# Short matrix products placed between long ones in a gated attention and MLP kernel

## The chip, the cores and the metric

The kernel runs on one core of one Trainium2 chip. The metric is the device time of one execution in microseconds (us). Before the change it is 208.64 us, the median of 3 runs (208.62 to 208.71). The profile shows one execution, which took 208.87 us; the span in its records, from first to last instruction, is 207.1 us.

## What is computed

Two branches over the same 2048 rows of 512 values are mixed by a gate per row. Branch A is linear attention with 32 heads of 16, whose features are softmaxes; branch B is a gated MLP whose second half is mixed over the rows.

```python
# A: B, S, D, H = 1, 2048, 512, 32; Dh = 16
q, k, v = split(x @ wqkv)                       # each (heads, 2048, 16)
pq, pk  = q @ w_phi, k @ w_phi                  # per head, 16 x 16
phi_q = concat([softmax(pq), softmax(-pq)])     # (heads, 2048, 32)
phi_k = concat([softmax(pk), softmax(-pk)])
kv  = einsum('bhsf,bhsd->bhfd', phi_k, v)       # the key sums
z   = einsum('bhsf->bhf', phi_k)
num = einsum('bhqf,bhfd->bhqd', phi_q, kv)      # the query sums
den = einsum('bhqf,bhf->bhq', phi_q, z)[..., None] + 1e-06
a   = (num / den) @ wo
# B: F = 1376, Fh = 688
zB = gelu(x @ w_in)
g  = w_sp @ layernorm(zB[..., Fh:]) + b_sp      # w_sp is 2048 x 2048
b  = (zB[..., :Fh] * g) @ w_out
gate = sigmoid((x * gate_w).sum(-1))
out  = gate * a + (1 - gate) * b
```

## The kernel before

The rows are cut into 16 tiles of 128. All matrix products accumulate in one PSUM tensor `ps` of 8 banks, each 128 x 512 in FP32. The order of work on every engine is the order in which the program writes it: there is no scheduler, each engine works through its own instructions in order and waits at semaphores where data is needed.

The stages, with their places in the profile:

1. Up to 59 us: x is transposed, branch B's `zz` (gelu) is formed with `z_piece` (line 180), the values `vv` with `v_proj` (line 282), and w_phi is folded into the key and query weights (`fold`, line 305).
2. 59 to 130 us, the key stage. `gg_half(i)` (line 396) makes half of one row tile of w_sp times zz: 16 products with 344 columns, into bank 0 or 1; VectorE then makes `u` from it (line 404), and a transposing DMA on SyncE's queue makes `uT`. `k_proj(t)` is four products of 512 columns (line 327), then two exponentials on ScalarE (line 333). `k_norm` calls `norm`: on VectorE a sum (line 338), a reciprocal (line 340) and a multiplication of one half (line 342), while GpSimd multiplies the other half. `kv_acc(t)` (line 372) is a block of 8 short products of 65 columns, one for each group of 4 heads, added over all tiles into eight slots (`slots`, banks 3 and 4).
3. 130 to 195 us, the query stage: a loop over `j` = 0 to 15. `gg_at` puts one or two `gg_half` ahead of j = 0, 1, 2, 3, 5, 7, 9, 11, 13 and 14. `q_num(j)` (line 420) is a block of 8 short products of 68 columns, written into the same `slots`; VectorE then takes a reciprocal of the denominators (`rd`, line 424) and writes the quotients times the gate (`o`, line 426), both reading all of `slots`; a transposing DMA makes `oT`. `q_proj(j + 4)` is like `k_proj`; `q_norm(j + 3)` is `norm` and a transposing DMA that makes `eT`, the stationary operand of a later `q_num`. From j = 3 on, `out_tile(j - 3)` adds six products with w_out (line 439) and four with wo (line 444), all of 512 columns; ScalarE copies the result to `ob` (line 448), which is then stored.
4. After the loop the last three out tiles. The very last one is made in two parts of 256 columns, in banks 6 and 7, each with its own copy and store.

There is one set of `slots`. So the first product of `q_num(j + 1)` waits until VectorE has finished `o` of j. In the program before, the loop's body is:

```python
gg(gg_at.get(j, 0))
q_num(j)                      # 8 short products, then rd and o on VectorE
if j + 4 < NT: q_proj(j + 4)
if j + 3 < NT: q_norm(j + 3)  # sum, reciprocal, multiplication on VectorE
if j >= LAG: out_tile(j - LAG)
```

Of the kernel before, what the change touches and what calls it, by code (L numbers as in the profile page):

```python
# [14 lines left out]
P = 128  # L15
S = 2048
D = 512
# [5 lines left out]
NT = S // P  # L23
NDT = D // P
# [6 lines left out]
NHG = 8  # L31
HW = 4 * DH
VP = HW + 2
QW = HW + 4
WSLOTS = 8
LAG = 3
# [3 lines left out]
def kernel(  # L40
# [14 lines left out]
    nc = tc.nc  # L55
# [9 lines left out]
    ps = psp.tile([P, 8, CH], FP32, name="ps")  # L65
# [5 lines left out]
    xT = pers.tile([P, NDT, S], BF16, name="xT")  # L71
    w_in = pers.tile([P, NDT, F + 1], BF16, name="w_in")
    wv = pers.tile([P, NDT, D], BF16, name="wv")
    wq = pers.tile([P, NDT, D], BF16, name="wq")
    wk = pers.tile([P, NDT, D], BF16, name="wk")
# [4 lines left out]
    vv = pers.tile([P, NT, NHG, VP], BF16, name="vv")  # L80
    wsp = pers.tile([P, WSLOTS, NT, P], BF16, name="wsp")
    kvx = pers.tile([P, NHG, QW], BF16, name="kvx")
# [59 lines left out]
    def load_wsp(t):  # L142
        nc.sync.dma_start_transpose(
            out=wsp[:, t % WSLOTS, :, :], in_=B_w_sp[t * P:(t + 1) * P, :]
        )
# [166 lines left out]
    KBANK = (2, 6)  # L312
    QBANK = (5, 7)
    ek_t = {}
    eq_t = {}
    w_in_flat = w_in[:].rearrange("p d f -> p (d f)")

    def e_slot(i):
        if i == 5:
            flat = xn[:].rearrange("p t d -> p (t d)")  # L320
        else:
            flat = w_in_flat[:, i * 2 * D:(i + 1) * 2 * D]
        return flat.rearrange("p (g a n) -> p g a n", g=NHG, a=2)

    def feat(t, w, b, e):
        for dt in range(NDT):
            nc.tensor.matmul(  # L327
                ps[:, b, :], lhsT=xT[:, dt, t * P:(t + 1) * P], rhs=w[:, dt, :],
                start=(dt == 0), stop=(dt == NDT - 1),
            )  # L330
        src = ps[:, b, :].rearrange("p (g n) -> p g n", g=NHG)
        for a, sc in enumerate((1.0, -1.0)):
            nc.scalar.activation(out=e[:, :, a, :], in_=src, func=AF.Exp, scale=sc)  # L333
# [12 lines left out]

    def k_proj(t):
        ek_t[t] = e_slot(t % 4)
        feat(t, wk, KBANK[t % 2], ek_t[t])

    def k_norm(t):
        norm(ek_t[t])

    def q_proj(t):
        eq_t[t] = e_slot(4 + t % 2 if t < 4 else (t - 4) % 6)
        feat(t, wq, QBANK[t % 2], eq_t[t])

    eT_t = {}

    def q_norm(t):  # L360
        e = eq_t.pop(t)
        norm(e)
        eT = wqkT[:, 2 * (t % 4):2 * (t % 4) + 2, :].rearrange("p a (b n) -> p (a b) n", n=P)
        nc.sync.dma_start_transpose(out=eT, in_=e.rearrange("p g a n -> p (g a n)"))
        eT_t[t] = eT

    slots = ps[:, 3:5, :].rearrange("p b (c w) -> p (b c) w", w=P)

    def kv_acc(t):
        ek = ek_t.pop(t)  # L370
        for g in range(NHG):
            nc.tensor.matmul(  # L372
                slots[:, g, 0:HW + 1], lhsT=ek[:, g, :, :].rearrange("p a n -> p (a n)"),
                rhs=vv[:, t, g, 0:HW + 1],
                start=(t == 0 and g % 4 == 0), stop=(t == NT - 1), skip_group_check=True,
            )

    def kv_extract():
        nc.vector.tensor_tensor(
# [9 lines left out]

    uT_t = {}  # L390

    def gg_half(i, s0=0, s1=NT):
        tt, h = divmod(i, 2)
        b = i % 2
        for s in range(s0, s1):
            nc.tensor.matmul(  # L396
                ps[:, b, 0:HF], lhsT=wsp[:, tt % WSLOTS, s, :],
                rhs=zz[:, s, FH + h * HF:FH + (h + 1) * HF],
                start=(s == 0), stop=(s == NT - 1),
            )  # L400
        if s1 < NT:
            return
        u = upad[tt % 3]
        nc.vector.scalar_tensor_tensor(  # L404
            out=u[:, h * HF:(h + 1) * HF], in0=ps[:, b, 0:HF], scalar=bcol[:, tt:tt + 1],
            in1=zz[:, tt, h * HF:(h + 1) * HF], op0=ALU.add, op1=ALU.mult,
        )
        if h == 1:
            uT = uTpool.tile([P, NFT, P], BF16, name="uT")
            nc.sync.dma_start_transpose(out=uT[:, :, :], in_=u[:, :])  # L410
            uT_t[tt] = uT
            if tt + WSLOTS < NT:
                load_wsp(tt + WSLOTS)

    oT_t = {}

    def q_num(t):
        eT = eT_t.pop(t)
        for g in range(NHG):
            nc.tensor.matmul(  # L420
                slots[:, g, 0:QW], lhsT=eT[:, g, :], rhs=kvx[:, g, :], start=True, stop=True
            )
        rd = ring2.tile([P, NHG, 4], FP32, name="rd")
        nc.vector.reciprocal(out=rd[:], in_=slots[:, :, HW:QW])
        o = ring2.tile([P, D], BF16, name="o")
        nc.vector.scalar_tensor_tensor(  # L426
            out=o[:].rearrange("p (g h d) -> p g h d", g=NHG, h=4),
            in0=slots[:, :, 0:HW].rearrange("p g (h d) -> p g h d", h=4),
            scalar=gate[:, t:t + 1],
            in1=rd[:, :, :, None].to_broadcast([P, NHG, 4, DH]), op0=ALU.mult, op1=ALU.mult,  # L430
        )
        oT = oTpool.tile([P, NDT, P], BF16, name="oT")
        nc.sync.dma_start_transpose(out=oT[:, :, :], in_=o[:, :])
        oT_t[t] = oT

    def out_part(t, b, n0, n1, ob, dma):
        uT, oT = uT_t[t], oT_t[t]
        for ft in range(NFT):
            nc.tensor.matmul(  # L439
                ps[:, b, n0:n1], lhsT=uT[:, ft, :], rhs=w_out[:, ft, n0:n1],  # L440
                start=(ft == 0), stop=False,
            )
        for g in range(NDT):
            nc.tensor.matmul(  # L444
                ps[:, b, n0:n1], lhsT=oT[:, g, :], rhs=wo[:, g, n0:n1],
                start=False, stop=(g == NDT - 1),
            )
        nc.scalar.activation(out=ob[:, n0:n1], in_=ps[:, b, n0:n1], func=AF.Copy)  # L448
        dma.dma_start(out=out2[t * P:(t + 1) * P, n0:n1], in_=ob[:, n0:n1])

    def out_tile(t):
        ob = ring3.tile([P, D], BF16, name="ob")
        if t < NT - 1:
            out_part(t, (2, 6)[t % 2], 0, D, ob, nc.scalar)
        else:
            out_part(t, 6, 0, D // 2, ob, nc.sync)
            out_part(t, 7, D // 2, D, ob, nc.scalar)

    uTpool = ctx.enter_context(tc.tile_pool(name="uTp", bufs=NT))
    oTpool = ctx.enter_context(tc.tile_pool(name="oTp", bufs=LAG + 2))  # L460
# [39 lines left out]
    for t in range(NT - VLAG, NT):  # L500
        v_proj(t)
    k_proj(0)
    k_proj(1)
    for t in range(NT - 5, NT):
        z1_gate(t)

    gg_next = 0

    def gg(n):
        nonlocal gg_next  # L510
        for _ in range(n):
            gg_half(gg_next)
            gg_next += 1

    Q_AT = {7: 0, 9: 1, 11: 2}
    for i in range(NT):
        gg(1)
        k_norm(i)
        if i >= 2:
            kv_acc(i - 2)  # L520
        if i + 2 < NT:
            k_proj(i + 2)
        if i in Q_AT:
            q_proj(Q_AT[i])
        if i - 1 in Q_AT:
            gg(1)
            q_norm(Q_AT[i - 1])

    q_proj(3)
    gg(2)  # L530
    kv_acc(NT - 2)
    kv_acc(NT - 1)
    kv_extract()
    gg_at = {0: 1, 1: 1, 2: 2, 3: 1, 5: 1, 7: 1, 9: 1, 11: 1, 13: 1, 14: 1}
    for j in range(NT):
        gg(gg_at.get(j, 0))
        q_num(j)
        if j + 4 < NT:
            q_proj(j + 4)
        if j + 3 < NT:  # L540
            q_norm(j + 3)
        if j >= LAG:
            out_tile(j - LAG)
    for j in range(NT - LAG, NT):
        out_tile(j)
# [28 lines left out]
```

## Time and profile before

| what | value |
|---|---|
| median time of 3 runs | 208.64 us (208.62 to 208.71) |
| the profiled execution's own time | 208.87 us |
| its span | 207.1 us, 1.8 us less than its own time |
| TensorE (PE) busy | 202.6 us, 98% of the span, 1399 products |
| VectorE (DVE) busy | 148.5 us, 72% |
| ScalarE (ACT) / GpSimd (POOL) busy | 82.1 us, 40% / 49.5 us, 24% |
| granted TensorE clock | 1.000 |
| short products, 65 and 68 columns | 128 and 128 |

The profile gives for each instruction its start and its duration. Products are pipelined: one has a duration from its start to its result of some 0.2 to 0.4 us, and the next begins long before that. What a product costs TensorE is the distance between two starts; the chain of waits shows this, since it lists how far each group moves the end. The chain's times of a product lie a fraction of a microsecond after the starts that the timeline shows. An instruction on VectorE that depends on nothing close before it can begin a little before the last one's end.

### The profile page before, as it was taken

What the parts mean: (1) busy time and instruction counts of PE and PEld (TensorE: products, weight loads), DVE (VectorE), ACT (ScalarE), POOL (GpSimd) and SP (SyncE); (2) the same over time, 40 slices, a digit from 0 to 9 for tenths busy, and PEclk for the clock granted to TensorE, in tenths of its full rate; (3) what the DMA queues carried; (4) which work ended last, traced back from release to release, by engine and by line L of the source; (5) the groups of instructions that cost most, each with busy time, mean ns of one, the idle gap of its engine ahead of it and who ended that gap; (6) DMA issues with size and microseconds to landing.
All of it is one profiled execution on the core that took longest, in us unless ns stands there. A gap on an engine that the chain in (4) does not pass through costs nothing.

```text
span 207.1 us, 3685 instructions
## 1 busy us (share of the span) xinstructions
PE 202.6 (98%) x1399; PEld 118.2 (57%) x1399; DVE 148.5 (72%) x304; ACT 82.1 (40%) x145; POOL 49.5 (24%) x46
## 2 busy tenths in 40 slices
PE   8899999999999999999999999999999999999994
PEld 7454555555455666666666667666455555555543
DVE  1048858376887988878888996698989778795500
ACT  3266757575684424250505102222524243341122
POOL 4000000000002343525352544032522252322000
DMA  6999899997000634472757771137765963567451
GB/s 188 233 188 255 178 178 227 173 188 234 0 3 0 138 69 112 101 127 67 162 118 112 139 170 41 38 90 76 170 140 119 151 162 80 134 135 164 101 104 51
DMA packets 90378, 26.50 MB, mean 128 GB/s; under 512 B 84168, under 2 KB 90360, under 8 KB 90360
## 3 DMA queue, kind: packets, MB, share of 16 engines
q1 hardware_dynamic: 87360, 23.84, 58.9%
q10 hardware_dynamic: 3000, 2.43, 3.9%
q8 instruction: 11, 0.18, 0.4%
q14 instruction: 7, 0.06, 0.1%
HBM read 3.44 MB, written 2.10 MB: 27 GB/s over the span
## 4 chain that ended last, share of the span: by engine, by line
PE 98%; issue 0%; ACT 0%; DVE 0%
PE ps L396 36%; PE ps L180 18%; PE ps L327 13%; PE ps L439 10%; PE ps L444 7%; PE ps L282 7%; PE ps L420 2%; PE ps L372 2%; PE ps L189 1%; PE ps L305 1%; PE ps L195 0%; ACT ob L448 0%; DVE w_in L212 0%; PE ps L209 0%
## 5 line engine op out<-in xcount | busy, mean ns | idle before, releaser
L396 PE MATMUL ps<-zz,wsp 128*128 128x344 bf16 x512 | 79.1, 310 | 0.0
L342 POOL TENSOR_TENSOR w_in<-w_in,rs 128x512 bf16<-128x512 bf16 x28 | 41.3, 1475 | 124.8 <-DVE rs L340 117.3
L396 PEld LDWEIGHTS <-wsp 128*128 128x128 bf16 x512 | 49.9, 98 | 27.9
L333 ACT ACTIVATE w_in<-ps 128x512 bf16<-128x512 f32 x56 | 30.1, 596 | 63.5 <-issue 21.5
L180 PE MATMUL ps<-w_in,xT 128*128 128x512 bf16 (+2 forms) x200 | 39.8, 350 | 0.7 <-DVE w_in L212 0.7
L338 DVE TENSOR_REDUCE zs<-w_in 128x64 f32<-128x1024 bf16 x28 | 33.8, 1209 | 0.0
L404 DVE SCALAR_TENSOR_TENSOR u<-ps,bcol,zz 128x344 bf16<-128x344 f32 x32 | 18.4, 574 | 18.6 <-PE ps L396 18.5
L180 PEld LDWEIGHTS <-xT 128*128 128x128 bf16 x200 | 18.9, 97 | 18.5 <-DMA w_in<-in_B_w_in_dram 1.0
L215 ACT ACTIVATE zz<-ps 128x1376 bf16<-128x1376 f32 (+2 forms) x18 | 21.4, 1190 | 18.9 <-PE ps L180 18.8
L439 PE MATMUL ps<-w_out,uT 128*128 128x512 bf16 (+1 forms) x102 | 23.5, 367 | 0.0
L224 DVE BATCH_NORM_STATS2 stats<-zz 128x6 f32<-128x344 bf16 x32 | 14.8, 505 | 11.2 <-ACT zz L215 11.2
L342 DVE TENSOR_TENSOR w_in<-w_in,rs 128x512 bf16<-128x512 bf16 x28 | 19.4, 692 | 1.0
L340 DVE RECIPROCAL rs<-zs 128x64 f32<-128x64 f32 x32 | 17.7, 552 | 3.2
L448 ACT ACTIVATE ob<-ps 128x512 bf16<-128x512 f32 (+1 forms) x17 | 9.7, 572 | 25.2 <-PE ps L444 23.7
L444 PE MATMUL ps<-wo,oT 128*128 128x512 bf16 (+1 forms) x68 | 16.6, 367 | 0.0
L327 PE MATMUL ps<-wq,xT 128*128 128x512 bf16 x64 | 16.4, 379 | 0.0
L327 PE MATMUL ps<-wk,xT 128*128 128x512 bf16 x64 | 16.2, 379 | 0.0
L327 PEld LDWEIGHTS <-xT 128*128 128x128 bf16 x128 | 10.8, 97 | 9.0
L282 PE MATMUL ps<-wv,xT 128*128 128x512 bf16 x64 | 15.6, 380 | 0.0
L439 PEld LDWEIGHTS <-uT 128*128 128x128 bf16 x102 | 9.7, 98 | 10.0
L426 DVE SCALAR_TENSOR_TENSOR o<-ps,st,rd 128x512 bf16<-128x512 f32 x16 | 12.0, 751 | 0.6
L444 PEld LDWEIGHTS <-oT 128*128 128x128 bf16 x68 | 6.7, 98 | 7.2
(56 smaller groups left out, 119.2 us busy)
## 6 DMA issues: line engine op xcount, KB each, us to landing
out_dram<-ob ACTq DMA_DIRECT2D x15, 128.0 KB, 1.9
w_out<-in_B_w_out_dram SPq DMA_DIRECT2D x1, 640.0 KB, 5.0
w_in<-in_B_w_in_dram SPq DMA_DIRECT2D x2, 256.0 KB, 4.1
wv<-in_A_wqkv_dram SPq DMA_DIRECT2D x1, 512.0 KB, 5.0
wo<-in_A_wo_dram SPq DMA_DIRECT2D x1, 512.0 KB, 5.4
w_in<-in_B_w_in_dram SPq DMA_DIRECT2D x1, 352.0 KB, 5.2
w_in<-in_B_w_in_dram ACTq DMA_DIRECT2D x2, 128.0 KB, 3.9
w_in<-in_B_w_in_dram SPq DMA_DIRECT2D x2, 128.0 KB, 3.5
```

Source lines behind the costliest of these rows:

```text
L180: nc.tensor.matmul(zb[:, n0:n1], lhsT=xT[:, dt, t * P:(t + 1) * P], rhs=w_in[:, dt, n0:n1], start=(dt == 0), stop=(dt == NDT - 1),)
L215: nc.scalar.activation(out=zz[:, t, n0:n1], in_=zbank(t)[:, n0:n1], func=AF.Gelu_apprx_tanh)
L282: nc.tensor.matmul(ps[:, b, :], lhsT=xT[:, dt, t * P:(t + 1) * P], rhs=wv[:, dt, :], start=(dt == 0), stop=(dt == NDT - 1),)
L327: nc.tensor.matmul(ps[:, b, :], lhsT=xT[:, dt, t * P:(t + 1) * P], rhs=w[:, dt, :], start=(dt == 0), stop=(dt == NDT - 1),)
L333: nc.scalar.activation(out=e[:, :, a, :], in_=src, func=AF.Exp, scale=sc)
L338: nc.vector.tensor_reduce(out=zs[:], in_=ev, axis=AX.X, op=ALU.add)
L340: nc.vector.reciprocal(out=rs[:], in_=zs[:])
L342: eng.tensor_tensor(out=ev[:, sl, :], in0=ev[:, sl, :], in1=rs[:, sl, None].to_broadcast([P, H, DH]), op=ALU.mult,)
L396: nc.tensor.matmul(ps[:, b, 0:HF], lhsT=wsp[:, tt % WSLOTS, s, :], rhs=zz[:, s, FH + h * HF:FH + (h + 1) * HF], start=(s == 0), stop=(s == ...
L404: nc.vector.scalar_tensor_tensor(out=u[:, h * HF:(h + 1) * HF], in0=ps[:, b, 0:HF], scalar=bcol[:, tt:tt + 1], in1=zz[:, tt, h * HF:(h + 1 ...
L439: nc.tensor.matmul(ps[:, b, n0:n1], lhsT=uT[:, ft, :], rhs=w_out[:, ft, n0:n1], start=(ft == 0), stop=False,)
L444: nc.tensor.matmul(ps[:, b, n0:n1], lhsT=oT[:, g, :], rhs=wo[:, g, n0:n1], start=False, stop=(g == NDT - 1),)
```

## The change

Three things are done.

1. The short products no longer stand in blocks of eight. In the key stage the eight of tile i - 2 go into `gg_half` of i, one behind each of its last eight products; those of tile 14 go into the last `gg_half` ahead of the query stage, and those of tile 15 stay a block. In the query stage, the eight of j go one behind each product of `q_proj(j + 4)` (four) and then of `out_tile(j - 3)`; for j below 3 the other four follow `q_proj` as a block, and from j = 12 on, where there is no `q_proj`, all eight go behind the first eight products of the out tile.
2. `q_num`, which now holds the division alone (`rd`, `o` and the transposing DMA of `oT`), is called at the end of the loop's body. On VectorE it stands behind the normalising `q_norm(j + 3)` and no longer ahead of it, and on SyncE's queue the DMA of `oT` stands behind that of `eT`.
3. The last out tile is made as 384 and 128 columns where it was 256 and 256.

The sizes and number of all other instructions stay. The diff's core:

```diff
-    def q_proj(t):
+    def q_proj(t, short=()):
+        short = list(short)
         eq_t[t] = e_slot(4 + t % 2 if t < 4 else (t - 4) % 6)
-        feat(t, wq, QBANK[t % 2], eq_t[t])
+        b = QBANK[t % 2]
+        for dt in range(NDT):
+            feat_mm(t, wq, b, dt)
+            if short:
+                short.pop(0)()
+        feat_exp(b, eq_t[t])
+        return short
...
-    def gg_half(i, s0=0, s1=NT):
+    def gg_half(i, short=()):
...
-        for s in range(s0, s1):
+        for s in range(NT):
             nc.tensor.matmul(
                 ps[:, b, 0:HF], lhsT=wsp[:, tt % WSLOTS, s, :],
                 rhs=zz[:, s, FH + h * HF:FH + (h + 1) * HF],
                 start=(s == 0), stop=(s == NT - 1),
             )
+            if s >= NT - len(short):
+                short[s - NT]()
...
+    def q_mm(t, g):
+        nc.tensor.matmul(
+            slots[:, g, 0:QW], lhsT=eT_t[t][:, g, :], rhs=kvx[:, g, :], start=True, stop=True
+        )
+
     def q_num(t):
-        eT = eT_t.pop(t)
-        for g in range(NHG):
-            nc.tensor.matmul(
-                slots[:, g, 0:QW], lhsT=eT[:, g, :], rhs=kvx[:, g, :], start=True, stop=True
-            )
         rd = ring2.tile([P, NHG, 4], FP32, name="rd")
         nc.vector.reciprocal(out=rd[:], in_=slots[:, :, HW:QW])
...
-    def out_part(t, b, n0, n1, ob, dma):
+    def out_part(t, b, n0, n1, ob, dma, short=()):
         uT, oT = uT_t[t], oT_t[t]
+        short = list(short)
         for ft in range(NFT):
             nc.tensor.matmul(
                 ps[:, b, n0:n1], lhsT=uT[:, ft, :], rhs=w_out[:, ft, n0:n1],
                 start=(ft == 0), stop=False,
             )
+            if short:
+                short.pop(0)()
...
-            out_part(t, 6, 0, D // 2, ob, nc.sync)
-            out_part(t, 7, D // 2, D, ob, nc.scalar)
+            out_part(t, 6, 0, D - P, ob, nc.sync)
+            out_part(t, 7, D - P, D, ob, nc.scalar)
...
     for i in range(NT):
-        gg(1)
+        gg(1, kv_short(i - 2) if i >= 2 else ())
         k_norm(i)
-        if i >= 2:
-            kv_acc(i - 2)
...
     for j in range(NT):
         gg(gg_at.get(j, 0))
-        q_num(j)
+        short = [lambda g=g: q_mm(j, g) for g in range(NHG)]
         if j + 4 < NT:
-            q_proj(j + 4)
+            short = q_proj(j + 4, short)
         if j + 3 < NT:
             q_norm(j + 3)
         if j >= LAG:
-            out_tile(j - LAG)
+            out_tile(j - LAG, short)
+        else:
+            for mm in short:
+                mm()
+        q_num(j)
```

More of the change, by code (lines that the diff above doesn't have):

```diff
@@ L323, in e_slot, with feat_mm, feat_exp @@
         return flat.rearrange("p (g a n) -> p g a n", g=NHG, a=2)
[L325 to L329, printed above, removed]
-            )
+    def feat_mm(t, w, b, dt):
+        nc.tensor.matmul(
+            ps[:, b, :], lhsT=xT[:, dt, t * P:(t + 1) * P], rhs=w[:, dt, :],
+            start=(dt == 0), stop=(dt == NDT - 1),
+        )
+    def feat_exp(b, e):
         src = ps[:, b, :].rearrange("p (g n) -> p g n", g=NHG)
@@ L348, in k_proj @@
         ek_t[t] = e_slot(t % 4)
-        feat(t, wk, KBANK[t % 2], ek_t[t])
+        b = KBANK[t % 2]
+        for dt in range(NDT):
+            feat_mm(t, wk, b, dt)
+        feat_exp(b, ek_t[t])
     def k_norm(t):
         norm(ek_t[t])
-    def q_proj(t):
+    def q_proj(t, short=()):
+        short = list(short)
         eq_t[t] = e_slot(4 + t % 2 if t < 4 else (t - 4) % 6)
-        feat(t, wq, QBANK[t % 2], eq_t[t])
+        b = QBANK[t % 2]
+        for dt in range(NDT):
+            feat_mm(t, wq, b, dt)
[3 more added lines that the diff above has]
+        return short
     eT_t = {}
@@ L367, with kv_mm @@
     slots = ps[:, 3:5, :].rearrange("p b (c w) -> p (b c) w", w=P)
+    def kv_mm(t, g):
+        nc.tensor.matmul(
+            slots[:, g, 0:HW + 1], lhsT=ek_t[t][:, g, :, :].rearrange("p a n -> p (a n)"),
+            rhs=vv[:, t, g, 0:HW + 1],
+            start=(t == 0 and g % 4 == 0), stop=(t == NT - 1), skip_group_check=True,
+        )
     def kv_acc(t):
-        ek = ek_t.pop(t)
         for g in range(NHG):
[L372 to L376, printed above, removed]
+            kv_mm(t, g)
     def kv_extract():
@@ L400, in gg_half @@
             )
-        if s1 < NT:
-            return
+            if s >= NT - len(short):
+                short[s - NT]()
         u = upad[tt % 3]
@@ L415 @@
     oT_t = {}
+    def q_mm(t, g):
+        nc.tensor.matmul(
+            slots[:, g, 0:QW], lhsT=eT_t[t][:, g, :], rhs=kvx[:, g, :], start=True, stop=True
+        )
     def q_num(t):
-        eT = eT_t.pop(t)
-        for g in range(NHG):
-            nc.tensor.matmul(
-                slots[:, g, 0:QW], lhsT=eT[:, g, :], rhs=kvx[:, g, :], start=True, stop=True
-            )
         rd = ring2.tile([P, NHG, 4], FP32, name="rd")
@@ L447, in out_part, with out_tile @@
             )
+            if short:
+                short.pop(0)()
         nc.scalar.activation(out=ob[:, n0:n1], in_=ps[:, b, n0:n1], func=AF.Copy)
         dma.dma_start(out=out2[t * P:(t + 1) * P, n0:n1], in_=ob[:, n0:n1])
-    def out_tile(t):
+    def out_tile(t, short=()):
         ob = ring3.tile([P, D], BF16, name="ob")
         if t < NT - 1:
-            out_part(t, (2, 6)[t % 2], 0, D, ob, nc.scalar)
+            out_part(t, (2, 6)[t % 2], 0, D, ob, nc.scalar, short)
         else:
-            out_part(t, 6, 0, D // 2, ob, nc.sync)
-            out_part(t, 7, D // 2, D, ob, nc.scalar)
+            out_part(t, 6, 0, D - P, ob, nc.sync)
+            out_part(t, 7, D - P, D, ob, nc.scalar)
     uTpool = ctx.enter_context(tc.tile_pool(name="uTp", bufs=NT))
@@ L507, with gg, kv_short @@
     gg_next = 0
-    def gg(n):
+    def gg(n, short=()):
         nonlocal gg_next
-        for _ in range(n):
-            gg_half(gg_next)
+        for k in range(n):
+            gg_half(gg_next, short if k == n - 1 else ())
             gg_next += 1
+    def kv_short(t):
+        return [lambda g=g: kv_mm(t, g) for g in range(NHG)]
     Q_AT = {7: 0, 9: 1, 11: 2}
     for i in range(NT):
-        gg(1)
+        gg(1, kv_short(i - 2) if i >= 2 else ())
         k_norm(i)
-        if i >= 2:
-            kv_acc(i - 2)
         if i + 2 < NT:
@@ L529 @@
     q_proj(3)
-    gg(2)
-    kv_acc(NT - 2)
+    gg(2, kv_short(NT - 2))
     kv_acc(NT - 1)
```

## The prediction

> **What bounds the kernel now.** I read the page's busy times and its chain first. TensorE is busy for 98% of the span, and the chain that ended last is TensorE for 98%: whatever makes TensorE wait or takes its time is paid in full, and nothing else counts unless it does that.
>
> ```profile
> PE 202.6 (98%) x1399; PEld 118.2 (57%) x1399; DVE 148.5 (72%) x304; ACT 82.1 (40%) x145; POOL 49.5 (24%) x46
> ...
> PE 98%; issue 0%; ACT 0%; DVE 0%
> ```
>
> Next the chain in order of time, where the query stage begins; columns are start, us, what.
>
> ```profile
> 131.85 0.25 PE ps L420 x8
> 132.10 0.86 PE ps L327 x4
> 132.97 2.33 PE ps L396 x16
> ```
>
> A short product costs 0.25 / 8 = 32 ns, one of 512 columns 0.86 / 4 = 216 ns, one of 344 columns 2.33 / 16 = 146 ns. Between 344 and 512 columns a column costs 70 / 168 = 0.42 ns, and 2 to 3 ns are fixed, so 65 and 68 columns alone would be 30 to 31 ns. The shorts of both stages are 256 x 32 = 8.2 us, with at most 256 x 1.6 = 0.4 us above their columns.
>
> Then the timelines of TensorE and VectorE around j = 7 (L420 at 162.14, a `gg_half` ahead of it) and j = 8 (165.42, none).
>
> ```profile
> 162.14 0.42 PE L420 MATMUL ps<-kvx,wqkT 128*128 128x68 bf16 x8
> 165.42 0.42 PE L420 MATMUL ps<-kvx,wqkT 128*128 128x68 bf16 x8
> ```
>
> ```profile
> 162.34 0.58 DVE L404 SCALAR_TENSOR_TENSOR u<-ps,bcol,zz 128x344 bf16<-128x344 f32 x1 [1.19 <-PE ps L396]
> 162.84 0.35 DVE L424 RECIPROCAL rd<-ps 128x32 f32<-128x32 f32 x1
> 163.22 0.75 DVE L426 SCALAR_TENSOR_TENSOR o<-ps,st,rd 128x512 bf16<-128x512 f32 x1
> 163.88 1.21 DVE L338 TENSOR_REDUCE zs<-w_in 128x64 f32<-128x1024 bf16 x1
> 165.20 0.55 DVE L340 RECIPROCAL rs<-zs 128x64 f32<-128x64 f32 x1
> 165.78 0.69 DVE L342 TENSOR_TENSOR w_in<-w_in,rs 128x512 bf16<-128x512 bf16 x1
> 166.39 0.35 DVE L424 RECIPROCAL rd<-ps 128x32 f32<-128x32 f32 x1
> 166.78 0.75 DVE L426 SCALAR_TENSOR_TENSOR o<-ps,st,rd 128x512 bf16<-128x512 f32 x1
> ```
>
> VectorE ends `o` of j = 7 at 163.97, and TensorE overwrites the slots at 165.42: 1.45 us to spare, because the normalising stands behind the division. VectorE runs at almost no idle here and at 166.39 is a microsecond behind the shorts of j = 8. That lag costs nothing today.
>
> **The division behind the normalising.** From start to start, `u` takes 0.50, the normalising 166.39 - 163.88 = 2.51, `rd` 0.39, and `o` ends 0.75 later. In the new order, `o` ends 0.50 + 2.51 + 0.39 + 0.75 = 4.15 us after `u` starts. A product that waits for VectorE starts 0.05 us after it: the gate column's copy ends at 9.35 + 0.17, the product starts at 9.58.
>
> ```profile
> 9.35 0.17 DVE L212 CAST w_in<-ps 128x4 bf16<-128x4 f32 x1 [4.36 <-PE ps L180]
> 9.58 0.91 PE L180 MATMUL ps<-w_in,xT 128*128 128x353 bf16 x5 [0.73 <-DVE w_in L212]
> ```
>
> So the slots are free 4.20 us after `u` starts, at 166.54. The first long product of j = 8 would start at 165.42 and its first short 0.216 later, at 165.64. That short waits 0.90 us; behind it in TensorE's order stand the rest of `q_proj`, the out tile and the next `gg_half`, so all of it is paid. The data of `rd` is no limit: the shorts of j = 7 are through 8 x 0.216 + 8 x 0.032 = 1.98 us after 162.14, and VectorE gets to `rd` only at 165.35. Adding up, with the delay so far in each start, from these rows of the two timelines:
>
> ```profile
> 131.89 0.58 DVE L404 SCALAR_TENSOR_TENSOR u<-ps,bcol,zz 128x344 bf16<-128x344 f32 x1 [1.54 <-PE ps L396]
> 135.14 0.42 PE L420 MATMUL ps<-kvx,wqkT 128*128 128x68 bf16 x8
> 141.12 0.58 DVE L404 SCALAR_TENSOR_TENSOR u<-ps,bcol,zz 128x344 bf16<-128x344 f32 x1 [0.57 <-PE ps L396]
> 144.37 0.42 PE L420 MATMUL ps<-kvx,wqkT 128*128 128x68 bf16 x8
> 147.65 0.42 PE L420 MATMUL ps<-kvx,wqkT 128*128 128x68 bf16 x8
> 192.69 0.42 PE L420 MATMUL ps<-kvx,wqkT 128*128 128x68 bf16 x8
> 195.10 0.42 PE L420 MATMUL ps<-kvx,wqkT 128*128 128x68 bf16 x8
> ```
>
>
> - j = 6, 8, 10, 12, each behind a j with a `gg_half`: 4 x 0.90 = 3.60.
> - j = 1: `u` at 131.89, slots free at 136.09; the short would start at 135.14 + 0.22: 0.73.
> - j = 2 has two `gg_half` ahead: none.
> - j = 3: VectorE starts `u` of the second half at 141.12 + 0.73 = 141.85, free at 146.05, against 144.37 + 0.73 + 0.22: 0.73.
> - j = 4: VectorE is through with `o` of j = 2 only at 146.00, overlapping the next `u` from 145.92, so free at 150.12, against 147.65 + 1.46 + 0.22: 0.79.
> - j = 15: there is no normalising, but the shorts of j = 14 now end only with the eighth long product of their out tile. The last starts 192.69 + 1.95 = 194.64, has its result 0.2 later, `rd` and `o` take 1.14, the signals 0.09: free at 196.07, against 195.10 + 0.22: 0.75.
> - j = 5, 7, 9, 11, 13, 14 have a `gg_half` of 2.33 us ahead, more than the lag: none. (After the wait at j = 8, `o` of j = 8 ends near 170.1, and the shorts of j = 9 come at 172.1.)
>
> Together 3.60 + 0.73 + 0.73 + 0.79 + 0.75 = 6.6 us. What gives this back? Nothing on TensorE: its work is the same. The SyncE queue issues `oT` behind `eT`, some 3 us later, and `oT` lands 2.4 us after that; its reader is the out tile three rounds on, at least 3 x 3.27 us away. For tile 15, `o` ends 1.4 us after the last short, plus 2.4 for the DMA, against 0.43 + 2 x 2.16 + 0.98 = 5.7 us of products ahead of the first with wo. GpSimd and ScalarE keep their order.
>
> **The shorts between long ones.** Each long product's weights now load while a short one streams. That is seen at every block's end: by single starts in the trace, a long comes 33.0 ns after a short on average (31 blocks), a short 31.9 after a short; a short after a long is at the long's own 146 or 216. I take 33.0 for the 205 shorts that newly stand ahead of a long one (7 in each of 15 key blocks and 13 query blocks, 3 in each of j = 0 to 2): 205 x 1.1 ns = +0.23 us. Strict alternation is not in the trace; the bounds are -0.4 (only the columns are paid) and +1.2 (5 ns more each, as the slowest short start shows: 37 ns against 32).
>
> The Trainium skill, in "TensorE: Matmul & The Clock Gate", section LDWEIGHTS, gives a weight load as columns / 1.2 ns, so 107 ns here, and Part 2 says that loads are pulled ahead of running products. Were shorts in a row held to that, 107 - 32 = 75 ns each would be there to hide, an estimate of 205 x 75 ns = 15 us of gain by the page against +0.23 us by the rows. The chain's 32 ns decides: the load is already hidden.
>
> In the key stage the shorts come up to eight long products (1.2 us) earlier and so ask earlier for normalised keys. For tile 0, GpSimd ends its half at 65.88 + 1.41 = 67.29, and the block started at 69.47: 2.2 us to spare, 1.0 left. For later tiles it is more. `u` comes 7 x 32 ns later in each half, beside VectorE's slack there. Cost nothing; if that cover were gone, tenths of a microsecond each.
>
> **The last out tile.** TensorE: 10 x 163 ns (384 columns by the line above) + 10 x 56 ns (the fold's 128 columns, four in 0.22) = 2.19, as the 20 x 109 of now. The last copy is of 128 columns, 0.28 us (line 206 has 128 x 128 at 0.272 to 0.277) in place of 0.38, and its product drains 0.05 sooner. The store is of 32 KB in place of 64 KB; I keep 1.5 us to landing. Sum -0.1, bounds -0.25 and +0.4 (1.9 us, what 128 KB take).
>
> "DMA: Bandwidth & Descriptors", Specifications, asks for at least 512 B per transfer, below which the DMA engine reads, modifies and writes. The rows stored last are now 256 B; no run here shows such a store, and the page gives no price for it.
>
> **Sum.** +6.6 + 0.23 - 0.1 = +6.7 us. The profiled execution goes from 208.87 to 215.6; the median of the runs lies 0.23 below it, so 215.4 us.
>
> **Rivals.**
> - A, faster: the division's wait does not bind, because VectorE's turn from `u` to the end of `o` fits into the 165.64 - 162.34 = 3.30 us that TensorE leaves it. That needs 0.9 us less than the rows add up to. Then only 0.4 and 0.1 to 0.25 are left: 208.1. Against it: 4.15 is a sum of measured starts in one order-bound engine. Chance 2%.
> - B, slower by less: the waits of the first rounds (1, 3, 4) or at 15 do not appear, since VectorE starts those rounds ahead; the four steady ones stay: 3.60 + 0.13, 212.4; or the division moves forward where I have it late. Chance 8%.
> - C, slower by more: alternation costs TensorE per product, or each wait drags its clock. For the clock, the hole of 0.73 us at 9.58 was followed by 353 columns at 149 ns each, full speed. Price: 205 x 20 ns = 4 us, 219.5. Chance 4%.
> - D: the shorts do not really move. The instruction order of the changed program has them between the long ones, each first one of j with a wait for VectorE. Chance 1%, 208.6.
>
> My forecast has the remaining 85%. Its own bounds are the tail's and the alternation's, and 0.1 us for each of the eight waits: 213.9 to 216.9. That leaves out A, most of B, C and D, so the range stands. A measurement of this kernel can tell 0.2% from no change. Chances: faster 2%, same 2%, slower 96%.
>
> **What would show it.** The profile after should list TensorE idle behind `o` (line 439 of the new file) with eight waits of 0.7 to 0.9 us, 6.6 in all, at j = 1, 3, 4, 6, 8, 10, 12 and 15, none in the key stage, and TensorE busy about as before. Shorts in the chain should cost 32 to 33 ns. If TensorE shows no wait for `o`, the forecast is wrong in its main step; if busy time grows, C holds.

## The result and the profile after

The changed kernel takes 214.84 us (median of 5 runs, 214.5 to 214.92) against 208.64 us (208.32 to 208.73) in the same set: +6.20 us, a ratio of 1.0295 with a 95% interval of 1.028 to 1.031. The forecast was 215.4 us, with a range of 213.9 to 216.9.

The page of the profile after: TensorE is still busy 96% of a longer span, but the chain that ended last is no longer its alone.

```profile
span 213.2 us, 3681 instructions
...
PE 204.2 (96%) x1399; PEld 118.2 (55%) x1399; DVE 148.7 (70%) x304; ACT 82.1 (39%) x145; POOL 49.5 (23%) x46
...
PE 84%; DVE 12%; issue 2%; ACT 0%; DVEq 0%
```

The waits of TensorE, all of them, first before and then after (columns: who for whom, us in total, times, longest). Before, none was for the slots:

```profile
PE ps L189 <- PEq L558: 0.8, 1, 0.8
PE ps L180 <- DVE w_in L212: 0.7, 1, 0.7
```

```profile
PE ps L431 <- DVE o L439: 5.3, 8, 0.7
PE ps L189 <- PEq L580: 0.8, 1, 0.8
```

Eight waits of the shorts (line 431) for the division's `o` (line 439), as many as forecast. The total of 5.3 is less than what they cost, because the profile counts a product as busy until its result is out. The cost is read from starts. Here are VectorE and TensorE behind the `gg_half` of j = 5, at the first short of j = 6:

```profile
155.35 0.58 DVE L417 SCALAR_TENSOR_TENSOR u<-ps,bcol,zz 128x344 bf16<-128x344 f32 x1 [2.08 <-PE ps L409]
155.84 1.21 DVE L339 TENSOR_REDUCE zs<-w_in 128x64 f32<-128x1024 bf16 x1
157.15 0.55 DVE L341 RECIPROCAL rs<-zs 128x64 f32<-128x64 f32 x1
157.74 0.69 DVE L343 TENSOR_TENSOR w_in<-w_in,rs 128x512 bf16<-128x512 bf16 x1
158.35 0.35 DVE L437 RECIPROCAL rd<-ps 128x32 f32<-128x32 f32 x1
158.73 0.75 DVE L439 SCALAR_TENSOR_TENSOR o<-ps,st,rd 128x512 bf16<-128x512 f32 x1
```

```profile
158.41 0.38 PE L326 MATMUL ps<-wq,xT 128*128 128x512 bf16 x1
159.54 0.19 PE L431 MATMUL ps<-kvx,wqkT 128*128 128x68 bf16 x1 [0.74 <-DVE o L439]
159.57 0.38 PE L326 MATMUL ps<-wq,xT 128*128 128x512 bf16 x1
```

`o` ends at 158.73 + 0.75 = 159.48, 4.13 us after `u` starts; the short starts 0.06 later. From the long product at 158.41 to the short are 1.13 us where 0.216 would do: 0.91 us lost. The profile calls 0.74 of it idle; the rest is what it lists of the long product, 0.38 us up to its result, beyond the 0.216 that the product costs. Taken in this way from single starts, the eight waits are 0.73 (j = 1), 0.73 (3), 0.78 (4), four times 0.91 (6, 8, 10, 12) and 0.75 (15): 6.6 us.

By stages, from the first product of the key stage (`k_proj(0)`), the first of j = 0 behind its `gg_half`, the first of the last out tile and the span's end, in us:

| kernel | before the key stage | key stage | query stage | last out tile and end |
|---|---|---|---|---|
| before | 59.02 | 72.67 | 70.14 | 5.30 |
| after | 58.86 | 72.51 | 76.63 | 5.17 |

Before the key stage nothing was changed; that it differs by 0.16 is the spread of the start between executions. The key stage gained 0.16, the query stage lost 6.49, which is 6.62 of waits less 0.13, and the end gained 0.13.

### The profile page after: what moved, and what is told of

Read it like the earlier page. It is cut to its first block, busy times and chain, and to the rows that moved or that the text cites. A ratio compares the mean times of both kernels' runs of the same rounds, so it can differ in the third digit from the quotient of the medians.

```text
span 213.2 us, 3681 instructions
## 1 busy us (share of the span) xinstructions
PE 204.2 (96%) x1399; PEld 118.2 (55%) x1399; DVE 148.7 (70%) x304; ACT 82.1 (39%) x145; POOL 49.5 (23%) x46
## 4 chain that ended last, share of the span: by engine, by line
PE 84%; DVE 12%; issue 2%; ACT 0%; DVEq 0%
PE ps L409 33%; PE ps L180 18%; PE ps L326 10%; PE ps L453 6%; PE ps L282 6%; PE ps L460 4%; DVE zs L339 4%; DVE o L439 3%; DVE rs L341 2%; DVE u L417 2%; PE ps L381 2%; PE ps L431 2%; PE ps L189 1%; DVE rd L437 1%; PE ps L305 1%
## 5 line engine op out<-in xcount | busy, mean ns | idle before, releaser
L409 PE MATMUL ps<-zz,wsp 128*128 128x344 bf16 x512 | 82.1, 309 | 0.0
L180 PE MATMUL ps<-w_in,xT 128*128 128x512 bf16 (+2 forms) x200 | 40.3, 357 | 0.0
L180 PEld LDWEIGHTS <-xT 128*128 128x128 bf16 x200 | 19.6, 100 | 17.7
L431 PE MATMUL ps<-kvx,wqkT 128*128 128x68 bf16 x128 | 22.9, 194 | 5.3 <-DVE o L439 5.3
L453 PE MATMUL ps<-w_out,uT 128*128 128x512 bf16 (+2 forms) x102 | 25.5, 367 | 0.0
L381 PE MATMUL ps<-vv,w_in 128*128 128x65 bf16 x128 | 21.7, 193 | 0.0
L326 PEld LDWEIGHTS <-xT 128*128 128x128 bf16 x128 | 11.6, 98 | 16.8 <-issue 5.7
L466 ACT ACTIVATE ob<-ps 128x512 bf16<-128x512 f32 (+2 forms) x17 | 9.7, 572 | 28.4 <-PE ps L460 26.8
L326 PE MATMUL ps<-wq,xT 128*128 128x512 bf16 x64 | 18.3, 379 | 0.0
L460 PE MATMUL ps<-wo,oT 128*128 128x512 bf16 (+2 forms) x68 | 16.8, 367 | 0.0
L453 PEld LDWEIGHTS <-uT 128*128 128x128 bf16 x102 | 9.2, 98 | 11.8 <-issue 1.9
```

The source lines that it names most:

```text
L180: nc.tensor.matmul(zb[:, n0:n1], lhsT=xT[:, dt, t * P:(t + 1) * P], rhs=w_in[:, dt, n0:n1], start=(dt == 0), stop=(dt == NDT - 1),)
L326: nc.tensor.matmul(ps[:, b, :], lhsT=xT[:, dt, t * P:(t + 1) * P], rhs=w[:, dt, :], start=(dt == 0), stop=(dt == NDT - 1),)
L381: nc.tensor.matmul(slots[:, g, 0:HW + 1], lhsT=ek_t[t][:, g, :, :].rearrange("p a n -> p (a n)"), rhs=vv[:, t, g, 0:HW + 1], start=(t == 0 ...
L409: nc.tensor.matmul(ps[:, b, 0:HF], lhsT=wsp[:, tt % WSLOTS, s, :], rhs=zz[:, s, FH + h * HF:FH + (h + 1) * HF], start=(s == 0), stop=(s == ...
L431: nc.tensor.matmul(slots[:, g, 0:QW], lhsT=eT_t[t][:, g, :], rhs=kvx[:, g, :], start=True, stop=True)
L453: nc.tensor.matmul(ps[:, b, n0:n1], lhsT=uT[:, ft, :], rhs=w_out[:, ft, n0:n1], start=(ft == 0), stop=False,)
```

## The experiments

The theory (W): the loss is TensorE waiting for slots that the division still reads, since the division now stands behind the normalising. Rivals: alternating products cost TensorE something themselves (P), for which the busy time speaks, 202.6 before and 204.2 after; or the late division costs in another way, through its transposing DMA or VectorE's load. Six kernels were run; their edits are shown shortened.

**Division ahead of the normalising, all else as in the change.**

```diff
     q_proj(j + 4, short)
-    q_norm(j + 3)
     out_tile(j - LAG, short)
     q_num(j)
+    q_norm(j + 3)
```

> The shorts stay between the long products, and only VectorE's order goes back: the division of j stands ahead of the normalising of j + 3. Theory W (the loss is TensorE waiting for slots that the late division still reads): the waits at j = 1, 3, 4, 6, 8, 10, 12 go, the one at j = 15 stays at 0.74 us, since there the shorts themselves end late; the alternation gives 0.35 us and the last tile 0.13, as the profile after shows them: 208.64 + 0.74 - 0.48 = 208.9 us. Rival P (the loss is what alternating products cost TensorE, whose listed busy time grew by 1.6 us): stays near 214.8.

Measured: 208.49 us against 208.35 of the kernel before, ratio 1.0008 (0.9997 to 1.002): 6 us came back by the order on VectorE alone, all but the wait at j = 15. In the query stage 70.78 us, 0.63 more than before. One wait is left in TensorE's timeline, the one at j = 15:

```profile
194.66 0.38 PE L453 MATMUL ps<-w_out,uT 128*128 128x512 bf16 x1
195.63 0.19 PE L431 MATMUL ps<-kvx,wqkT 128*128 128x68 bf16 x1 [0.59 <-DVE o L439]
```

0.97 from start to start, so 0.75 lost, as summed. P falls: the shorts alternate here as in the change. Of the 1.6 us more busy time, 8 x 0.16 = 1.3 us are the listed ends of the long products in front of the waits, and no work.

**Division behind the normalising, all else as before.**

```diff
-    q_num(j)            # 8 shorts, then the division
+    q_block(j)          # the 8 shorts
     q_proj(j + 4)
     q_norm(j + 3)
     out_tile(j - LAG)
+    q_num(j)            # the division
```

> The kernel before with one thing changed: the division of j stands behind the normalising of j + 3; the shorts stay blocks and the last tile 256 and 256. W: the block comes 0.216 us earlier against the division than an alternating short does, so seven waits of 0.95, 0.95, 0.78 and four of 1.12 us, none at j = 15: 7.2 us, 215.8 us, slower than the whole change. P: no loss, 208.6.

Measured: 215.55 us against 208.35, ratio 1.0348 (1.0334 to 1.0362), which is +7.2 us as forecast.

The list of TensorE's waits, and the first short of j = 6 in the timeline:

```profile
PE ps L419 <- DVE o L427: 6.0, 7, 1.0
```

```profile
159.55 0.41 PE L419 MATMUL ps<-kvx,wqkT 128*128 128x68 bf16 x8 [0.95 <-DVE o L427]
```

Seven waits; from starts they are 0.94, 0.94, 0.77 and four of 1.12, 7.1 us. This one move makes the loss by itself. The alternation, in the change, makes six of these seven waits shorter by one long product (not that at j = 4, 0.77 here and 0.78 there) and adds the one at j = 15.

**The same order as in the change, with two sets of slots.**

```diff
+    slots_b = ps[:, 6:8, :].rearrange("p b (c w) -> p (b c) w", w=P)
+    def q_slots(t): return slots_b if t % 2 else slots
...
-    b = QBANK[t % 2]                              # q_proj
+    b = QBANK[t % 2] if t < 4 else 5
...
-    out_part(t, (2, 6)[t % 2], 0, D, ...)
+    out_part(t, (2, 5)[t % 2] if t >= 9 else 2, 0, D, ...)
```

(q_mm, rd and o use `q_slots(t)`; the last tile's two parts are in banks 5 and 3.)

> The whole change with VectorE's order as changed (division behind the normalising), but odd j use a second set of slots in banks 6 and 7, so that a short waits for the division of j - 2 and no longer of j - 1; q_proj and the out tiles give up their second bank for it. W: no wait on TensorE at all, 208.64 - 0.48 = 208.2 us. A rival in which the late division itself costs (its transposing DMA late on SyncE's queue, or VectorE being the bound): near 214.8.

Measured: 208.06 us against 208.35, ratio 0.998 (0.9967 to 0.9992). The order on VectorE and on TensorE is the one that cost 6.6 us of waits, and TensorE waits for nothing in the key and query stages; the only wait in its list is the one at the start:

```profile
PE ps L189 <- PEq L584: 0.8, 1, 0.8
```

How this looks in the round behind one with a `gg_half`, at the first short of j = 8, and on VectorE at the same time:

```profile
164.93 0.38 PE L326 MATMUL ps<-wq,xT 128*128 128x512 bf16 x1
165.14 0.19 PE L435 MATMUL ps<-kvx,wqkT 128*128 128x68 bf16 x1
```

```profile
165.25 0.75 DVE L443 SCALAR_TENSOR_TENSOR o<-ps,st,rd 128x512 bf16<-128x512 f32 x1
```

The short starts at 165.14, before `o` of j = 7 has begun at 165.25. So the late division costs nothing in itself; it was the sharing of the slots that made it cost.

**Only the multiplication of the normalising behind the division.**

```diff
     short = q_proj(j + 4, short)
-    q_norm(j + 3)       # sum, reciprocal, multiplication
+    q_norm_a(j + 3)     # sum, reciprocal, GpSimd's half
     out_tile(j - LAG, short)
     q_num(j)
+    q_norm_b(j + 3)     # VectorE's half, transposing DMA
```

> As the whole change, but VectorE's multiplication of the normalising (0.61 us from start to start) stands behind the division; sum and reciprocal stay ahead. W, by the same sum with 0.61 less ahead of the division: waits of 0.12 (j = 1, 3), 0.78 (j = 4, where VectorE is late from the round before), 0.29 four times, 0.74 (j = 15), 2.9 us together, 208.64 + 2.9 - 0.48 = 211.1 us. P: as the whole change, 214.8.

Measured: 209.72 us against 208.35, ratio 1.007 (1.0056 to 1.0084), +1.4 us: the direction is right, but the expected +2.5 is 1 us too much. The starts show six waits and not eight: 0.72 (j = 4), four of 0.13 and 0.75 (15), 2.0 us. VectorE's timeline, in the round of j = 6, says why:

```profile
153.86 1.21 DVE L351 TENSOR_REDUCE zs<-w_in 128x64 f32<-128x1024 bf16 x1
155.18 0.55 DVE L353 RECIPROCAL rs<-zs 128x64 f32<-128x64 f32 x1
155.64 0.29 DVE L465 RECIPROCAL rd<-ps 128x32 f32<-128x32 f32 x1
155.97 0.75 DVE L467 SCALAR_TENSOR_TENSOR o<-ps,st,rd 128x512 bf16<-128x512 f32 x1
```

In the change, `rd` starts 158.35 - 157.15 = 1.20 us after the reciprocal; here 0.46, and `o` 0.33 after `rd` and no longer 0.38. So 0.79 us went, not 0.61. The reciprocal's step of 0.59 in my sum held a wait of the multiplication for its result; `rd` does not need that result and begins before the reciprocal is out, which is 0.13. The other 0.05 is `rd` itself, which lasts 0.29 us here and 0.35 in the change; why is open. With 0.79 in place of 0.61 the steady wait is 0.91 - 0.79 = 0.12, where 0.13 was measured, and those at j = 1 and 3 vanish.

**Division first, and the shorts of j = 14 as a block.**

```diff
     short = [lambda g=g: q_mm(j, g) for g in range(NHG)]
+    if j == NT - 2:
+        for mm in short: mm()
+        short = []
```

(on top of the first experiment)

> As the first experiment (division ahead of the normalising, shorts between long products), and the eight shorts of j = 14 stand again as a block ahead of their out tile, so that the division of j = 14 can start 1.7 us sooner. W: no wait for the slots is left; alternation and last tile remain: 208.6 - 0.35 - 0.13 = 208.1 us, 0.2% under the kernel before, as with two sets of slots but with one set. Rival: the wait at j = 15 has another cause than the shorts' late end and stays: 208.9.

Measured: 208.18 us against 208.40, ratio 0.9985 (0.9975 to 0.9996). The wait at j = 15 is gone, because the division of j = 14 starts behind the block and not behind eight long products. The timelines of TensorE (block of j = 14, first short of j = 15) and of VectorE (`o` of j = 14):

```profile
192.14 0.42 PE L431 MATMUL ps<-kvx,wqkT 128*128 128x68 bf16 x8
...
194.55 0.38 PE L453 MATMUL ps<-w_out,uT 128*128 128x512 bf16 x1
194.77 0.19 PE L431 MATMUL ps<-kvx,wqkT 128*128 128x68 bf16 x1
```

```profile
193.22 0.75 DVE L439 SCALAR_TENSOR_TENSOR o<-ps,st,rd 128x512 bf16<-128x512 f32 x1
```

`o` ends at 193.97, 0.80 us before the short. This kernel and the one with two sets of slots both beat the kernel before, by 0.2 and 0.3 us, where 0.5 was expected of each; which is the faster of the two cannot be told from these intervals. By the stages in the table below, both are 0.40 us shorter from the key stage on, 0.13 of it by the last tile.

**The last out tile alone.**

```diff
-    out_part(t, 6, 0, D // 2, ob, nc.sync)
-    out_part(t, 7, D // 2, D, ob, nc.scalar)
+    out_part(t, 6, 0, D - P, ob, nc.sync)
+    out_part(t, 7, D - P, D, ob, nc.scalar)
```

> The kernel before with the last out tile as 384 and 128 columns and nothing else. From the two profiles (first product of the last tile to the end of the span 5.30 us before, 5.17 after): -0.13 us, 208.5, too little for the times to tell; in the profile 5.17 us again. Rival: the smaller store lands later and the part costs time, +0.3 or more.

Measured: 208.26 us against 208.40, ratio 0.9987 (0.9977 to 0.9996). In the profile, 5.17 us from the last tile's first product to the end, as in the change; the rival's +0.3 is not there. The two stores land in 1.7 us (96 KB) and 1.5 us (32 KB, rows of 256 B), in the list of DMA issues by kind, size and us to landing. Those of the kernel before stand first, the new ones behind them:

```profile
out_dram<-ob SPq DMA_DIRECT2D x1, 64.0 KB, 1.6
out_dram<-ob ACTq DMA_DIRECT2D x1, 64.0 KB, 1.5
```

```profile
out_dram<-ob SPq DMA_DIRECT2D x1, 96.0 KB, 1.7
...
out_dram<-ob ACTq DMA_DIRECT2D x1, 32.0 KB, 1.5
```

The stages of those that had no wait or one, beside the kernel before (us):

| kernel | key stage | query stage | last out tile and end |
|---|---|---|---|
| before | 72.67 | 70.14 | 5.30 |
| division first | 72.51 | 70.78 (one wait, 0.75) | 5.17 |
| division first, block at 14 | 72.51 | 70.04 | 5.17 |
| two sets of slots | 72.51 | 70.03 | 5.17 |
| last tile alone | 72.67 | 70.14 | 5.17 |

## Why the prediction was right, and where it was not

*The division behind the normalising, +6.6 us.* Right in cause, place and size: the same eight rounds, none in the key stage, and each wait within 0.02 us of its sum. The cause is shown from both sides: the order alone on the old kernel costs 7.2 us; taking away the order gives back seven of the eight waits, 5.9 us, and taking away the shared slots gives back all eight. The wait at j = 15, 0.75 of the 6.6, is not the order's: there the shorts end late, as the prediction has it, and the block at j = 14 removes it.

*What could give it back: nothing.* Right: with two sets of slots the late `oT` costs nothing.

*The shorts between long ones, +0.23 us.* Wrong in sign. The step that failed took the start of a long product after a block, 33.0 ns behind the last short, as the price of a short in alternation. In alternation the long product follows, by single starts, 29.2 ns after a short of 65 columns and 30.0 ns after one of 68 on average, in all profiles that alternate; the long before a short takes about 1 ns more than its own. The chain of the profile after shows a short and a long in turn in the key stage; 0.35 us for two such pairs are 175 ns for 146 and 29:

```profile
69.16 0.03 PE ps L381
69.19 0.15 PE ps L409
69.34 0.03 PE ps L381
69.37 0.14 PE ps L409
69.51 0.03 PE ps L381
```

Without waits the two stages together came out 0.16 + 0.10 to 0.11 = 0.27 us shorter than before (two sets of slots, and block at 14), on the side of the bound of -0.4 for paying columns alone. So 0.27 of the 0.4 us between the blocks and their columns were to be had, 0.27 / 205 = 1.3 ns for each of the shorts moved.

*The last tile, -0.1 us.* Right: -0.13 to -0.15 in all six profiles that have it. The store of 256 B rows (32 KB) landed in 1.5 us, as that of 512 B rows (64 KB) before; the rule of the Trainium skill that I had set beside it ("DMA: Bandwidth & Descriptors", Specifications, at least 512 B) shows no price in this kernel, where the store is small.

*Against the weight-load rule.* By the estimate from the figure of the Trainium skill ("TensorE: Matmul & The Clock Gate", section LDWEIGHTS), the alternation would have been a gain of 15 us; the row of 32 ns per short said that the load was hidden already, and 0.27 us is what the runs gave. The profile before has a row for the loads themselves, which the prediction left out (busy us in total, mean ns of one):

```profile
L420 PEld LDWEIGHTS <-wqkT 128*128 128x128 bf16 x128 | 6.2, 98 | 2.4
```

A load is listed with 98 ns, near the page's 107, but 128 of them fill 6.2 us and not 12.5: inside a block they begin some 32 ns apart, one over the other. So the length of a load is not what a short costs.

*The sum.* +6.7 was forecast, +6.2 measured. Of the 0.5 between them, the alternation's sign is 0.23 + 0.27 = 0.50.

*The rivals.* A, that the wait does not bind, is what the two kernels that lift it show: its price was 0.5 us under the kernel before, and they lie 0.3 and 0.2 under it. In the changed kernel it had no room. B and C fall with the eight waits at their full sums and with TensorE's pace in alternation: the 512 columns after a wait take 0.216 us as elsewhere, so the holes of 0.9 us did not slow it. D falls with the timeline, where shorts and long products alternate.

## What to carry to other kernels

When a step is moved behind another on an engine that works in order, look for who waits for its release of a buffer and not only for its result: here the result had three rounds of slack, and the buffer 1.45 us against 2.51 us of normalising put ahead of its release. Add up the starts of the instructions from the last one that has to wait to the end of the release, and compare that with what the bounding engine leaves; the difference is the price. Here it was right to 0.02 us for each wait. When a step is taken out of such a sum, take its handover with it: the next instruction may not depend on what the last one had waited for.

## What the runs showed of the hardware that was not expected

- A short product in strict alternation with long ones costs 29.2 ns (65 columns) and 30.0 ns (68), in a block 31.9. With the 1 ns more of the long ahead of it, alternation comes to the 30 to 31 ns of its columns.
- An instruction on VectorE that does not depend on the one before it starts 0.08 to 0.09 us before that one's end (reciprocal at 155.18 for 0.55, `rd` at 155.64). One that does depend starts 0.03 to 0.04 us after it (157.15 + 0.55, 157.74), and behind the sum mostly 0.10 to 0.11 (153.86 + 1.21, 155.18).
- The part ahead of the key stage, the same program in all kernels, ended at times from 58.27 to 59.02 us in eight profiles. A difference of 0.7 us between two spans can be that alone; the stages' own lengths repeated to 0.02 us where their program was the same and nothing waited.
